# Normalised blocks at every second gate/up pair instead of at every pair, and two weight loads moved behind them

## The chip, the cores and the metric

One core of a Trainium2 chip runs the kernel. The metric is the device time of one execution in microseconds (us); of several executions the median is quoted.

In profile lines PE is TensorE and PEld its weight loads, DVE VectorE, ACT ScalarE, POOL GpSimd, and SPq the queue that issues DMA transfers. A line of a timeline gives start and length in us; a line of a group gives the busy time in us and, behind it, the mean ns of one instruction. `ps` is PSUM, to which TensorE writes its results, and `SB` is SBUF, the other memory of the core. Taking a result out of PSUM is called an evacuation.

## The reference, cut to what matters

A block of linear attention and a gated feed-forward block share one normalised input of 2048 tokens by 1024 features.

```python
xn = _layernorm(x)
pq, pk = phi(q), phi(k)                      # q, k, v = split(xn @ wqkv), 32 heads
kv, z = einsum(pk, v), einsum(pk)
num, den = pq @ kv, pq @ z + 1e-6
s = (num / den) @ wo
g = silu((silu(xn @ w_gate) * (xn @ w_up)) @ w_down)    # w_gate, w_up: 1024 x 3584
return x + s * g
```

The kernel divides not the product but phi(q) by its denominator, ahead of the product. This is "normalising PQ".

## The kernel before: the parts that matter here

The kernel lists its operations in program order; a scheduler written in the kernel then picks the order on each of five queues from modelled times and sets all semaphores. Its model lets a VectorE operation without an input in PSUM start only when GpSimd is free (`if o.port: when = max(when, free["pool"])`), but it adds no semaphore for that. After the q, k and v stage come 28 gate/up *pairs* (14 slices of the weights, each with two halves of the tokens; TensorE works 11.49 us on one), then the s stage and the d stage (down projection). Everything is multiplied by Strassen's scheme, so besides TensorE much adding and subtracting is to be done: VectorE and ScalarE take results out of PSUM, GpSimd combines the weights of coming slices.

PQ lies in eight blocks (token half `p`, a further half `j`, four of the eight head groups). One block is normalised so:

```python
def normalise(p, j, half):
    RBs = [tmp(F2), tmp(F2)]
    ...
    for hl in range(4):                 # reciprocals of the denominators, from DRAM
        ...  dma(...).pad = 3.0
    for g2 in range(2):
        RB = RBs[g2]
        for gl in range(2):             # four times: ScalarE scales, VectorE multiplies
            ...
            act([z_r] + [...], [RB], zr, zr, ACT.Identity, 512, "sb", scale=zc[:, g:g + 1])
            tt([sr, RB], [sr], src.bitcast(FP16), src, zr, ALU.mult, 512, True, NE[half])
    ...
    dma([SB.reg(o, 4 * KB)], [...], q_scr[p, half, j], ...)     # the block back to DRAM
```

The pairs, and what is listed with them:

```python
order = [(n, p) for n in range(12) for p in range(2)] + [(12, 0), (13, 0), (12, 1), (13, 1)]
norm = {N0 + q: [(q % 4 // 2, q % 2, q // 4)] for q in range(8)}        # N0 = 4
...
for z, (n, p) in enumerate(order):
    ...
    gu_pair(p, n, G[n], at)
    ...
    if z == N0 + 9:                     # down weights, into the room that PQ had
        wd_load("A10", 30.0)
        wd_load("A11", 30.0)
    if p == 0 and n < 12:               # once in two pairs: load and combine weights
        while wk[0] - 2 <= n + NA:
            next_load()                 # slice n + 2: DMA, then GpSimd
        G[n + 1].inner(IE, JG)          # GpSimd
    ...
    for a in norm.get(z, ()):
        normalise(*a)
```

So pair z is the first of the two that share a slice where z is even, and the second where z is odd, up to pair 23.

## Time and profile before

| | before |
|---|---|
| median of the runs beside the prediction | 744.12 us (740.38 to 744.96) |
| span of the profiled execution | 741.6 us |
| TensorE busy in the span | 706.9 us |

In the timeline of TensorE, kernel before (start, length), the figures in brackets are the idle time just before a stretch and what ended it.

```profile
257.26 1.91 PE L427 MATMUL ps<-SB 128*128 128x256 f16 x12 [1.78 <-ACT SB L477]
260.23 17.52 PE L427 MATMUL ps<-SB 128*128 128x512 f16 x112 [1.06 <-DVE ps L485]
279.18 11.32 PE L427 MATMUL ps<-SB 128*128 128x256 f16 x70 [1.43 <-DVE SB L485]
291.09 19.69 PE L427 MATMUL ps<-SB 128*128 128x256 f16 x128 [0.59 <-DVE SB L485]
...
333.35 148.76 PE L427 MATMUL ps<-SB 128*128 128x256 f16 x958 [1.29 <-ACT ps L477]
```

### The profile page before, as it was taken

To read this page: it belongs to the slowest core of one execution; us is meant where nothing else is said; L and a number is where in the kernel's file an instruction comes from. 1 tells how busy PE (TensorE), PEld (TensorE's weight loads), DVE (VectorE), ACT (ScalarE), POOL (GpSimd) and SP (SyncE) were. 2 spreads that over 40 slices of the span, in tenths; PEclk is the share of its full clock that TensorE was granted. 3 is DMA by queue.
4 is the path that set the end of the run, shared out by engine and by line. 5 is a ranking of instruction groups with operands and counts; after the bars stand their busy time and mean duration, and the time that the engine had idled before them with its cause. 6 is when DMAs were issued, how large, how long until landed. Compare 5 with 4: busy or idle time off the path is not lost.

```text
span 741.6 us, 11805 instructions
## 1 busy us (share of the span) xinstructions
PE 706.9 (95%) x4219; PEld 399.4 (54%) x4247; DVE 560.0 (76%) x1099; ACT 374.0 (50%) x729; POOL 286.2 (39%) x258
## 2 busy tenths in 40 slices
PE   8999999988899899999999999999999999999996
PEld 3444445544466555556666666666554456464642
DVE  6988776968977889888777777779878966556433
ACT  4777755976646576665455454454565112121211
POOL 2011000336558765983979767732840000000000
PEclk9999999999999999999999999999999999999999
DMA  9344245130233455358531334345699256573522
GB/s 302 99 81 102 44 113 170 59 114 4 78 102 97 135 178 190 121 159 287 174 100 46 112 93 121 94 130 163 213 278 282 87 171 186 168 206 95 184 72 71
DMA packets 142235, 101.58 MB, mean 137 GB/s; under 512 B 19040, under 2 KB 137056, under 8 KB 142176
## 3 DMA queue, kind: packets, MB, share of 16 engines
q1 hardware_dynamic: 142176, 100.82, 45.4%
q8 instruction: 33, 0.54, 0.3%
q14 instruction: 26, 0.21, 0.1%
HBM read 68.16 MB, written 29.49 MB: 132 GB/s over the span
## 4 chain that ended last, share of the span: by engine, by line
PE 73%; DVE 15%; DMA 6%; ACT 3%; issue 2%; SPq 0%; DVEq 0%; ACTq 0%
PE ps L427 73%; DVE SB L485 8%; ACT SB L477 3%; DMA SB<-h_scratch 2%; DMA SB<-SB 2%; DVE ps L485 2%; DVE SB L1041 1%; DVE SB L1048 1%; DMA SB<-in_A_x_dram 1%; DMA SB<-q_scratch 1%; DVE stats L1001 1%; ACT ps L477 1%; DVE stats L1002 1%; SPq L497 0%; DVE SB L1213 0%
## 5 line engine op out<-in xcount | busy, mean ns | idle before, releaser
L427 PE MATMUL ps<-SB 128*128 128x256 f16 (+4 forms) x4098 | 697.5, 331 | 24.8 <-ACT ps L477 7.0
L427 PEld LDWEIGHTS ps<-SB 128*128 128x128 f16 (+1 forms) x4126 | 393.7, 98 | 326.1 <-DVE ps L485 14.6
L485 POOL TENSOR_TENSOR SB<-SB 128x512 f16<-128x512 f16 (+5 forms) x224 | 272.2, 1250 | 200.8 <-PE ps L427 77.9
L477 ACT ACTIVATE SB<-ps 128x256 f32<-128x256 f32 (+5 forms) x443 | 233.8, 562 | 169.4 <-PE ps L427 154.6
L485 DVE TENSOR_TENSOR SB<-SB 128x512 f16<-128x512 f16 (+9 forms) x332 | 206.7, 658 | 58.6 <-ACT SB L477 18.6
L485 DVE TENSOR_TENSOR SB<-ps,SB 128x512 f16<-128x512 f32 (+2 forms) x318 | 182.0, 593 | 68.6 <-PE ps L427 53.0
L485 DVE TENSOR_TENSOR ps<-ps,SB 128x512 f32<-128x512 f32 (+1 forms) x250 | 128.2, 528 | 34.6 <-PE ps L427 28.1
L477 ACT ACTIVATE ps<-ps 128x512 f32<-128x512 f32 (+1 forms) x172 | 84.4, 491 | 104.8 <-PE ps L427 98.0
L477 ACT ACTIVATE SB<-SB 128x512 f16<-128x512 f32 (+1 forms) x68 | 42.2, 621 | 81.3 <-DVE SB L485 81.2
L1005 POOL TENSOR_TENSOR rstd<-veps,neg_half 128x1 f32<-128x1 f32 x16 | 11.4, 724 | 65.5 <-DVE veps L1004 64.3
L1041 DVE TENSOR_SCALAR SB<-SB 128x512 f16<-128x512 f16 x64 | 22.1, 353 | 9.3 <-ACT SB L477 9.3
L477 ACT ACTIVATE SB<-SB,zc 128x512 bf16<-128x512 bf16 x32 | 22.0, 717 | 4.5 <-DVE SB L485 3.7
L477 ACT ACTIVATE SB<-SB,nmr,rstd 128x1024 f16<-128x1024 bf16 x12 | 14.7, 1237 | 1.3 <-DVE nmr L1007 1.1
L1001 DVE BATCH_NORM_STATS2 stats<-SB 128x6 f32<-128x512 bf16 x16 | 11.0, 686 | 3.4 <-DMA SB<-in_A_x_dram 3.4
L1048 DVE SCALAR_TENSOR_TENSOR SB<-SB 128x512 bf16<-128x512 f32 x15 | 12.5, 843 | 0.0
L1002 DVE BATCH_NORM_STATS2 stats<-SB 128x6 f32<-128x512 bf16 x16 | 10.9, 681 | 0.0
L427 PE MATMUL ps<-SB,ident 128*128 128x512 f16 x17 | 5.7, 496 | 1.4 <-POOL ident L508 1.4
L1048 DVE SCALAR_TENSOR_TENSOR SB<-ps,SB 128x512 bf16<-128x512 f32 x9 | 6.1, 686 | 0.0
L456 PE MATMUL ps<-ident,SB 128*128 128x128 f16 x40 | 3.1, 220 | 2.3 <-DVE SB L1011 1.6
L456 PEld LDWEIGHTS ps<-ident,SB 128*128 128x128 f16 x40 | 2.4, 98 | 4.3 <-DVE SB L1011 2.8
L1298 DVE RECIPROCAL SB<-SB 128x64 f32<-128x64 f32 x8 | 4.4, 547 | 0.1
L427 PEld LDWEIGHTS ps<-SB,ident 128*128 128x128 f16 x17 | 1.9, 121 | 4.2 <-issue 2.2
(28 smaller groups left out, 23.5 us busy)
## 6 DMA issues: line engine op xcount, KB each, us to landing
h_scratch<-SB SPq DMA_DIRECT2D x112, 128.0 KB, 2.7
SB<-h_scratch SPq DMA_DIRECT2D x16, 896.0 KB, 6.2
SB<-in_B_w_gate_dram SPq DMA_DIRECT2D x14, 512.0 KB, 4.1
SB<-in_B_w_up_dram SPq DMA_DIRECT2D x14, 512.0 KB, 5.3
SB<-in_B_w_down_dram SPq DMA_DIRECT2D x4, 1792.0 KB, 9.0
SB<-in_A_wqkv_dram SPq DMA_DIRECT2D x12, 512.0 KB, 7.1
SB<-in_A_x_dram SPq DMA_DIRECT2D x16, 256.0 KB, 3.0
SB<-r_scratch SPq DMA_DIRECT2D x32, 128.0 KB, 2.8
```

Of the source, the lines that this page charges most:

```text
L427: last = h.matmul(o() if callable(o) else o, l() if callable(l) else l, r() if callable(r) else r, start=st, stop=sp, skip_group_check=True)
L456: last = h.transpose(o(), i(), ident[:, :])
L477: return op("act", reads, writes, lambda h: h.activation(ev(o), ev(i), func, **kw), n / 1200.0 + (0.055 if src == "ps" else 0.095) + (0.09 ...
L485: f = lambda h: h.tensor_tensor(ev(o), ev(a), ev(b), alu)
L1001: dve([xr] + ([named("ve", 0)] if q == 1 else []), [sA], lambda h: h.bn_stats(stats[:, j, 0, :], xa[:, 0:512]), 512)
L1002: dve([xr] + ([named("ve", 0)] if q == 1 else []), [sB], lambda h: h.bn_stats(stats[:, j, 1, :], xa[:, 512:1024]), 512)
L1005: pool([ver, nh_r], [rsr], lambda h: h.tensor_tensor(rstd[:, j, :], veps[:, j, :], neg_half[:, :], ALU.pow), 0.56)
L1041: dve([e], [e], lambda h: h.tensor_scalar(vap(e, FP16), vap(e, FP16), 1.0, EPS_PHI, ALU.min, ALU.add), 512, 3.84, urgent=PU).port = True
L1048: dve(reads + [e], [out_r], lambda h: h.scalar_tensor_tensor(out_ap, ev(src), 0.0, vap(e, FP16), ALU.max, ALU.add), 512, urgent=PU).port = ...
L1298: dve([ea], [ra], lambda h, q=q: h.reciprocal(vap(ra, F32)[:, q * 64:q * 64 + 64], vap(ea, F32)[:, q * 64:q * 64 + 64]), 400)
```

## The change

The intent is to thin out the extra work of VectorE and ScalarE: each block has two pairs to itself. The down weights, which take PQ's place, can then only be loaded later.

```diff
-    N0, NA, WA, QU, ZD = 4, 2, True, 20.0, 2
+    N0, NA, WA, QU, ZD, NS = 4, 2, True, 20.0, 2, 2
...
-        norm = {N0 + q: [(q % 4 // 2, q % 2, q // 4)] for q in range(8)}
+        norm = {N0 + NS * q: [(q % 4 // 2, q % 2, q // 4)] for q in range(8)}
...
-            if z == N0 + 9:
+            if z == N0 + NS * 7 + 2:
```

## The prediction

> **What bounds the kernel now.** I read the page first (who is busy), then the busy times by stretch, then TensorE's waits, and last the timelines of VectorE, GpSimd and the DMA queue side by side, because the question is what comes just before a TensorE gap. In the page, TensorE is the bound:
>
> ```profile
> PE 706.9 (95%) x4219; PEld 399.4 (54%) x4247; DVE 560.0 (76%) x1099; ACT 374.0 (50%) x729; POOL 286.2 (39%) x258
> ```
>
> The multiplications stay the same under the change, so all it can win is TensorE's idle time, 741.6 - 706.9 = 34.7 us in the whole span, and only the part that normalisation causes. The first line of the next block is the stretch that holds all eight normalised blocks (pairs 4 to 11, from the first reload of the reciprocals at 232 to the last stores at 336), the second the rest of the gate/up stage without them. The columns are busy time and count by engine:
>
> ```profile
> 232.00:338.00 106.00, 99.08 (x634) 60.94 (x633) 91.23 (x168) 68.85 (x134) 76.63 (x61) 1.00 0.49 155
> 338.00:440.00 102.00, 102.00 (x659) 64.27 (x657) 76.02 (x144) 49.96 (x107) 76.01 (x61) 1.00 0.45 141
> ```
>
> TensorE is full without the normalising and loses 6.92 us with it, at the same clock. The waits of TensorE in the first stretch add up to 2.0 + 1.8 + 1.8 + 1.3 = 6.9 us and all name VectorE or ScalarE; in the second there are none:
>
> ```profile
> PE ps L427 <- DVE SB L485: 2.0, 2, 1.4
> PE ps L427 <- DVE ps L485: 1.8, 3, 1.1
> PE ps L427 <- ACT SB L477: 1.8, 1, 1.8
> PE ps L427 <- ACT ps L477: 1.3, 1, 1.3
> ```
>
> A second measure that does not rely on modelled matmul ends is the issue of each gate weight, once for every two pairs, which waits for a buffer that TensorE gives back. Start, length, engine:
>
> ```profile
> 237.30 0.40 SPq L497 DMA_DIRECT2D SB<-in_B_w_gate_dram  x1
> 337.52 0.38 SPq L497 DMA_DIRECT2D SB<-in_B_w_gate_dram  x1
> 360.51 0.38 SPq L497 DMA_DIRECT2D SB<-in_B_w_gate_dram  x1
> 383.49 0.38 SPq L497 DMA_DIRECT2D SB<-in_B_w_gate_dram  x1
> ```
>
> Without normalising two pairs take 22.99 us (360.51 - 337.52; 22.98 for the next). From 237.30 to 337.52 there are four such periods in 100.22 us; 4 x 22.985 = 91.94. The loss is **8.28 us**, a little more than the visible idle time. That is what stands to be won.
>
> Why does normalising cost so much? Its 32 VectorE multiplications are one row of the list of groups in that stretch:
>
> ```profile
> L485 DVE TENSOR_TENSOR SB<-SB 128x512 f16<-128x512 bf16 x32 | 25.2, 822 | 0.0
> ```
>
> 822 ns is a mean of two very different cases. Single ones, in order of time (VectorE), and below them GpSimd's busy stretches:
>
> ```profile
> 239.50 0.75 DVE L485 TENSOR_TENSOR SB<-SB 128x512 f16<-128x512 bf16 x2
> 241.23 0.41 DVE L485 TENSOR_TENSOR SB<-SB 128x512 f16<-128x512 bf16 x1
> ...
> 252.47 3.25 DVE L485 TENSOR_TENSOR SB<-SB 128x512 f16<-128x512 bf16 x2
> 257.36 2.20 DVE L485 TENSOR_TENSOR SB<-SB 128x512 f16<-128x512 bf16 x2
> ```
>
> ```profile
> 227.77 10.40 POOL L485 TENSOR_TENSOR SB<-SB 128x1024 f16<-128x1024 bf16 x10
> 244.66 15.43 POOL L485 TENSOR_TENSOR SB<-SB 128x1024 f16<-128x1024 bf16 x11 [6.48 <-DMA SB<-in_B_w_up_dram]
> ```
>
> Block one (pair 4) falls at 239.5 to 242.3, where GpSimd is idle (238.17 to 244.66, waiting for the next up weights): 0.38 to 0.42 us each. Block two (pair 5) falls into GpSimd's 15.43 us stretch: 5.45 us for four. Over all eight blocks I count 16 multiplications in GpSimd's idle time, 6.24 us together (0.39 each), and 16 in its stretches, 18.96 us (1.19 each); the sum is the row's 25.2. Every one of the seven TensorE gaps (257.26, 260.23, 279.18, 291.09, 311.02, 311.95, 333.35) ends within about 5 us of a slow group (252.47, 257.36, 274.95, 286.95, 308.14, 328.19); no gap follows the fast groups of 239.5, 267.9, 292.6 to 295.3 and 335.3 before a slow one.
>
> **What the Trainium skill says.** "SBUF — State Buffer", section "Who interferes with whom": a VectorE instruction with two SBUF inputs contends with a GpSimd instruction that reads SBUF, and the one that issues second blocks fully until the first is through. The trace agrees: 0.39 us against 1.19 us for one form, split by whether GpSimd works. The same section has it that VectorE operations with at most one SBUF input do not contend, which fits the evacuations out of PSUM keeping their length with and without normalising (128x512 f32 to f16: 684 ns in the first stretch, 688 in the second). "VectorE: DVE Perf Modes", section "The perf-mode tier table", gives tensor_tensor on 16-bit SBUF operands the 2x mode and any PSUM operand 1x; 0.39 us here against 0.69 us for the PSUM form of the same size agrees in order. "Perfetto Trace Analysis", section "Per-instruction lifecycle", note on the GPSIMD instruction, warns that a GpSimd span is unreliable; I use only where its stretches begin and end, and the VectorE lengths confirm them.
>
> **The change part by part.** Nothing is added or removed: 8 blocks of 4 reciprocal reloads (128 KB each), 4 ScalarE scalings, 4 VectorE multiplications and one 512 KB store before and after; and two down loads of 1792 KB each.
>
> *Normalising at pairs 4, 6, ..., 18.* (a) Average load. A pair takes 11.49 us. Without a block VectorE does 8.5 us in it (17.02 in 360 to 383, halved) and ScalarE 5.7. A block adds 4 x 0.717 = 2.9 us on ScalarE and 1.6 to 6 us on VectorE. Before, eight pairs in a row carry one; VectorE was busy 91.23 of 106 us (86%) with the backlog handed from pair to pair. After, each loaded pair is followed by an empty one. (b) Position, which I hold to be the larger part. All even pairs are the first of their two, and GpSimd repeats its work once for every two. The instruction order of the changed kernel shows it: on the DMA queue each of the eight blocks has one and the same place, reloads, gate, two stores, up, one store, then the store of the normalised block, before GpSimd's combination of the just issued weights. This is the position of block one in the kernel before (reloads 231.96, gate 237.30, up 238.85, store 242.34). In the later stretch without normalising GpSimd ends a short group at 386.11 and starts the next weights at 390.69, with the gate issued at 383.49; the block should fall at about 385.7 to 388.8, idle but for perhaps the end of one 1.16 us operation. So the 32 multiplications should take 32 x 0.39 = 12.5 us instead of 25.2, and 8.5 + 1.6 = 10.1 of 11.49 us on VectorE, 5.7 + 2.9 = 8.6 on ScalarE in a loaded pair. That such a pair costs TensorE nothing is not only argued: from 232 to 247 the kernel before carries block one, and TensorE is busy 15.00 of 15.00 us. Gain on the path: the 8.28 us.
>
> *Down loads with pair twenty.* They must wait for the last normalised store, as the loaded bytes take its place. Before, one was issued between the gate and up weights and the other behind them (338.18 and 346.21), and the combination on GpSimd started only at 350.68, 13.2 us after the gate, against 7.2 normally; TensorE still had no gap. After, both lie three stores ahead of the gate of pair 24, about 10 us (418 to 429 in the old times). At the 279 to 288 GB/s moved by the DMA around 340, 3.67 MB take about 13 us, so the weights come some 3 us late: less than the 6 before, which cost nothing. They are first used in the s stage, well over 50 us later. Effect 0.
>
> *Later stages.* The s and d stages only start earlier. Their instruction order changes in a few places near the end; TensorE has 0.5 us of waits after 534 and cannot win there. I allow 0 to 1 us loss.
>
> Sum: -8.3 + 0 + 0.3 = -8 us; 744.1 - 8 = 736.
>
> **The rivals.** (1) The slow multiplications stay: what counts is that a block meets GpSimd's long work, and the scheduler's modelled times put it a few us off. For it: its margin is about 2 us. Against: block one and the repeated order. Then half of them or more are slow, gaps fall only through the lower average load, and I would see 740 to 742. (2) Average load alone is the cause and position is incidental: the gain would be about the same if an empty pair clears each backlog, but the multiplications would stay near 0.8 us. (3) The down loads back to back fill the queue, the stores of h behind them hold their buffers, and pairs 20 to 23 stall: 338.18 and later show one store waiting 3.33 us to be issued, yet no gap; 1 to 3 us lost, 737 to 739. (4) The gain is hidden again, as the s stage waits for transfers (3.9 and 4.6 us for q_scratch in the chain). Against: those loads are released by buffers that the same TensorE stream frees, so they move with it. If wrong, 739 to 744.
>
> **Range and chances.** The three times of before differ by 4.6 us, with the median near the top, so 736 has about 1.5 us of doubt from that alone; (1), (3) and (4) lengthen the upper side, nothing makes the gain much greater than the 8.3 us. I give 733 to 740.5. Faster by over 2% needs 729.2, a gain of 14.9 us, almost twice what this stage loses: 0.02. Slower by over 2% needs a new wait of 15 us: 0.01. Within 2%: 0.97.
>
> **What would show it.** Right: gate issues 23.0 us apart through pairs 4 to 19, no TensorE waits there, the 32 multiplications at 12 to 14 us in all, TensorE full from about 204 to 468, and later stages of the same length. Wrong: multiplications still near 800 ns (position failed); periods of over 23.5 us; a gap at pairs 20 to 23 beside the down loads; or a longer span from the last gate issue to the end.

## The result, and the profile after

The changed kernel took 734.01 us (731.7 to 736.4, 4 runs) against 743.46 us of the kernel before in the same rounds. The ratio is 0.9878, with a 95% interval of 0.9833 to 0.9924. A ratio here is the mean time of one kernel's runs over that of the other's of the same rounds, so not quite the ratio of the medians. Two more sets of runs gave 0.9904 and 0.9887; the mean of the three is 0.989, which is 8.2 us of 743.

Of the kernel after, in the order in which the prediction looked at the kernel before: the busy line of the page; the stretch from the first to the last block (busy time and count on TensorE, weight load, VectorE, ScalarE and GpSimd); the row of the 32 multiplications.

```profile
PE 705.0 (97%) x4247; PEld 400.0 (55%) x4247; DVE 546.9 (75%) x1099; ACT 372.3 (51%) x729; POOL 283.2 (39%) x258
```

```profile
228.00:404.00 176.00, 176.00 (x1137) 111.11 (x1136) 137.34 (x278) 105.86 (x215) 131.56 (x106) 1.00 0.45 142
```

```profile
L485 DVE TENSOR_TENSOR SB<-SB 128x512 f16<-128x512 bf16 x32 | 12.6, 415 | 0.0
```

TensorE is never idle while blocks are normalised, at the same granted clock of 1.00 as before, and the multiplications take half of what they took, with nothing changed in the instruction itself. One block on VectorE, and the stretches of GpSimd ahead of and behind it:

```profile
258.09 0.75 DVE L485 TENSOR_TENSOR SB<-SB 128x512 f16<-128x512 bf16 x2
259.82 0.42 DVE L485 TENSOR_TENSOR SB<-SB 128x512 f16<-128x512 bf16 x1
260.48 0.42 DVE L485 TENSOR_TENSOR SB<-SB 128x512 f16<-128x512 bf16 x1
```

```profile
239.94 17.56 POOL L485 TENSOR_TENSOR SB<-SB 128x1024 f16<-128x1024 bf16 x14 [6.17 <-DMA SB<-in_B_w_up_dram]
262.75 17.56 POOL L485 TENSOR_TENSOR SB<-SB 128x1024 f16<-128x1024 bf16 x14 [5.24 <-DMA SB<-in_B_w_up_dram]
```

GpSimd is idle from 257.50 (239.94 + 17.56) to 262.75, and the block lies from 258.09 to 260.90. The eight blocks follow each other at 22.98 to 22.99 us, and none of the 32 multiplications overlaps a GpSimd operation. Gate issues on the DMA queue:

```profile
232.91 0.40 SPq L497 DMA_DIRECT2D SB<-in_B_w_gate_dram  x1
255.89 0.40 SPq L497 DMA_DIRECT2D SB<-in_B_w_gate_dram  x1
...
439.76 0.38 SPq L497 DMA_DIRECT2D SB<-in_B_w_gate_dram  x1
```

Two pairs now take 22.98 us from the first block on. From 232.91 to the last gate issue it is 206.85 us; in the kernel before, the same distance (237.30 to 452.44) is 215.14 us. The difference is 8.29 us.

Read the spans with care. The profiled executions are 12.0 us apart (741.6 and 729.6), more than the change made. The table splits them at the first block's gate issue and at the last gate issue. The third column is another execution of the changed kernel.

| us | before | after | after, second set |
|---|---|---|---|
| start to the first block's gate issue | 237.30 | 232.91 | 237.32 |
| from there to the last gate issue | 215.14 | 206.85 | 206.85 |
| from there to the end | 289.1 | 289.8 | 291.2 |

The first row differs by 4.4 us between two executions of one kernel, before any instruction that was moved; the last by 1.4 us. A part of the 4.4 us goes with the clock: in 120 to 180 us it was 1.00 in the execution of the second column and 0.97 in the other two, by estimate 1.8 us (0.03 of 60 us). The rest is not explained. Only the middle row repeats to 0.01 us, and it holds the effect.

### The profile page after: what moved, and what is told of

It is laid out like the page before. It is cut to its first block, busy times and chain, and to the rows that moved or that the text cites.

```text
span 729.6 us, 11830 instructions
## 1 busy us (share of the span) xinstructions
PE 705.0 (97%) x4247; PEld 400.0 (55%) x4247; DVE 546.9 (75%) x1099; ACT 372.3 (51%) x729; POOL 283.2 (39%) x258
## 4 chain that ended last, share of the span: by engine, by line
PE 80%; DVE 8%; DMA 6%; ACT 3%; issue 1%; SPq 0%; DVEq 0%
PE ps L427 80%; DVE SB L485 4%; DMA SB<-h_scratch 3%; ACT SB L477 2%; DMA SB<-in_A_x_dram 1%; DMA SB<-q_scratch 1%; DVE SB L1041 1%; DVE ps L485 1%; DVE SB L1048 1%; DMA out_dram<-SB 1%; ACT ps L477 1%; SPq L497 0%; DMA SB<-SB 0%; DVE SB L1213 0%; DVE stats L1001 0%
## 5 line engine op out<-in xcount | busy, mean ns | idle before, releaser
L427 PE MATMUL ps<-SB 128*128 128x512 f16 (+4 forms) x4126 | 695.6, 330 | 15.6 <-ACT ps L477 4.7
L485 POOL TENSOR_TENSOR SB<-SB 128x512 f16<-128x512 f16 (+5 forms) x224 | 269.2, 1238 | 193.9 <-DMA SB<-in_B_w_up_dram 85.1
L485 DVE TENSOR_TENSOR SB<-SB 128x512 f16<-128x512 f16 (+9 forms) x332 | 193.1, 615 | 56.8 <-ACT SB L477 20.9
```

The lines of the kernel that those rows point to most:

```text
L427: last = h.matmul(o() if callable(o) else o, l() if callable(l) else l, r() if callable(r) else r, start=st, stop=sp, skip_group_check=True)
L485: f = lambda h: h.tensor_tensor(ev(o), ev(a), ev(b), alu)
```

## The experiments

Two theories stood against each other at the start. *Position*: a block costs TensorE time where its multiplications run beside GpSimd's work. *Load*: what counts is that a loaded pair is followed by an empty one. A third claim was that the down loads matter. Twelve runs were made, in three sets of four; the ratio is to the kernel before of the same set.

| run | what | median us | ratio (95% interval) | 32 multiplications, us |
|---|---|---|---|---|
| after_again | the changed kernel | 735.30 | 0.9904 (0.9879 to 0.993) | 12.7 |
| odd_pairs | blocks at pairs 5, 7, ..., 19 | 748.86 | 1.0084 (1.0059 to 1.0109) | 33.8 |
| two_per_even | two blocks at 4, 6, 8, 10 | 751.31 | 1.0118 (1.009 to 1.0147) | 24.5 |
| load_only | before, down loads at pair 20 | 743.85 | 1.0012 (0.9978 to 1.0045) | 24.8 |
| before_memset | before, GpSimd reads nothing | 725.69 | 0.9771 (0.9747 to 0.9794) | 12.2 |
| after_memset | after, GpSimd reads nothing | 724.77 | 0.9754 (0.973 to 0.9778) | 12.6 |
| six_on | blocks at pairs 6, 8, ..., 20 | 733.06 | 0.9877 (0.9851 to 0.9902) | 12.6 |
| load_late | after, down loads at pair 26 | 735.38 | 0.9901 (0.9875 to 0.9927) | 12.6 |
| odd_memset | odd_pairs, GpSimd reads nothing | 725.02 | 0.9763 (0.9736 to 0.9789) | 12.0 |
| two_memset | two_per_even, GpSimd reads nothing | 725.29 | 0.9769 (0.9746 to 0.9793) | 12.3 |
| xe2_pool | after, four more operations on GpSimd | 741.98 | 1.0 (0.9971 to 1.003) | 12.6 |
| after_third | the changed kernel | 734.11 | 0.9887 (0.9865 to 0.991) | 12.6 |

**The changed kernel as a control**, in two of the sets; no edit.

> Control, the changed kernel beside the variants. Every theory: ratio to the kernel before about 0.988 (some 734 against 743 us), no TensorE gap between the first and the last normalised block, the 32 multiplications 12.6 us together, gate issues 22.98 us apart.

> Control beside the three: ratio to the kernel before 0.986 to 0.993.

Both ratios came as expected.

**The same spread, at odd pairs** (edit to the changed kernel):

```diff
-    N0, NA, WA, QU, ZD, NS = 4, 2, True, 20.0, 2, 2
+    N0, NA, WA, QU, ZD, NS = 5, 2, True, 20.0, 2, 2
```

> Same spread over sixteen pairs, but each block at the second pair of its two (pairs 5, 7, ..., 19), down loads with pair 21. Position theory (a block must meet GpSimd's idle time): the multiplications fall into GpSimd's 17.56 us stretch, take 25 to 38 us together, TensorE gaps return, time 737 to 743. Load theory (an empty pair after each loaded one is enough): no gaps whatever the multiplications cost, time as the changed kernel, 733 to 735.

The spread is as wide as in the changed kernel, yet it was slower than the kernel before, and slower than even the position theory had it: 748.86 us. One block of it, on GpSimd, VectorE and TensorE in turn:

```profile
268.43 15.45 POOL L485 TENSOR_TENSOR SB<-SB 128x1024 f16<-128x1024 bf16 x11 [5.55 <-DMA SB<-in_B_w_up_dram]
```

```profile
276.52 2.98 DVE L485 TENSOR_TENSOR SB<-SB 128x512 f16<-128x512 bf16 x2
279.42 1.34 DVE L485 TENSOR_TENSOR SB<-ps,SB 128x256 f32<-128x256 f32 x3
```

```profile
280.89 23.43 PE L427 MATMUL ps<-SB 128*128 128x256 f16 x148 [1.36 <-ACT ps L477]
```

Two multiplications take 2.98 us instead of 0.75 inside GpSimd's stretch; the evacuations behind them on VectorE begin at 279.42. ScalarE's next two scalings waited 0.89 and 0.57 us for VectorE, so its evacuation too comes late (280.46), and TensorE, which by the profile waits for that one, stands for 1.36 us. The same gap follows every one of the eight blocks, 1.03 to 1.89 us. By the gate issues (236.45 to 434.98) eight periods take 198.53 us against 8 x 22.98 = 183.84: a loss of 14.7 us with 24 slow multiplications, where the kernel before loses 8.3 with 16. The load theory alone is refuted: an empty pair behind each loaded one saved nothing here.

**Two blocks at each of four even pairs** (edit to the changed kernel):

```diff
-        norm = {N0 + NS * q: [(q % 4 // 2, q % 2, q // 4)] for q in range(8)}
+        norm = {N0 + NS * q: [(r % 4 // 2, r % 2, r // 4) for r in (2 * q, 2 * q + 1)] for q in range(4)}
```

> Two blocks in each of pairs 4, 6, 8 and 10, none in the odd ones: the mean load of the kernel before with the position of the changed one. Position theory: the first block of a pair fast, the second running late into GpSimd's stretch, multiplications 14 to 20 us together, time 735 to 739. Load theory: two blocks on one pair are worse or no better than one on each, time 742 to 747.

Both expectations were missed: 751.31 us. The scheduler did not keep the second block in the pair; it let multiplications run on into GpSimd's stretch (three at 250.76 took 3.62 us, four at 272.15 took 4.71). Four periods, 235.49 to 346.71, took 111.22 us against 91.92, a loss of 19.3 us, though the multiplications together were no slower than in the kernel before. Their sum is thus no measure of the loss. The four periods, and below them the same four of two_memset (told of further down), with the length, then TensorE's busy time, and its granted clock third from the end:

```profile
235.49:346.71 111.22, 101.16 (x594) 59.53 (x593) 87.06 (x161) 64.53 (x128) 71.56 (x56) 0.92 0.45 144
```

```profile
227.86:320.51 92.65, 92.65 (x594) 57.09 (x593) 75.11 (x161) 64.38 (x128) 30.51 (x56) 1.00 0.55 172
```

For the same 594 matmuls TensorE was idle for 10.1 us (four gaps of 1.96 to 3.29) and busy for 8.5 us more, at a mean clock of 0.92: nearly half of the loss is TensorE at a lower clock, which was 0.64 to 0.71 in the 5 us from 255, 275, 305 and 340, around the ends of the four gaps. In odd_pairs, with gaps of at most 1.89 us, and in the kernel before the clock was 1.00 through the blocks. What lowers it is not shown.

**Only the down loads moved** (edit to the kernel before):

```diff
-            if z == N0 + 9:
+            if z == 20:
```

> The kernel before with only its two down loads moved to pair 20. Position and load theory: nothing, ratio to the kernel before 0.997 to 1.003 (743 us), gate issues as uneven as before between pairs 4 and 11. If the move of the loads gave a part of the gain: 735 to 741.

Nothing, as expected: 1.0012. The profile has the old gaps in the old places, for instance

```profile
257.24 1.91 PE L427 MATMUL ps<-SB 128*128 128x256 f16 x12 [1.14 <-ACT SB L477]
```

**The cause taken away.** In the kernel before and the changed one, and later in the two variants, every tensor_tensor of GpSimd was made a memset of the same output. Order, semaphores and all places stay; the result is wrong.

```diff
             if eng == "pool":
+                f = lambda h: h.memset(ev(o), 0.01)
                 return op("pool", reads, writes, f, n / 531.0 + 0.2)
```

> The kernel before, with every GpSimd tensor_tensor replaced by a memset of the same output (wrong result on purpose): same instruction order, semaphores and places of the blocks, but GpSimd reads nothing. Contention as cause: the 32 multiplications fall from 25.2 to about 12.5 us although one block still lies in every pair, the TensorE gaps between 232 and 337 go, and the time is within 1.5 us of the changed kernel with the same memsets. Load theory: VectorE's backlog comes from eight loaded pairs in a row, so gaps of some us stay and the time is at least 4 us above the changed kernel with memsets.

> The changed kernel with the same memsets (wrong result on purpose). Every theory: multiplications 12.5 us, no gaps in the gate/up stage, time as the changed kernel within 2 us (733 to 736).

> The odd-pair variant with every GpSimd tensor_tensor replaced by a memset (wrong result on purpose): blocks in the same places, GpSimd reads nothing. Contention as the cause of the loss of 1.0 to 1.9 us per block: all eight gaps go, multiplications about 12.5 us, time within 1.5 us of the changed kernel with memsets (some 725 us, ratio 0.974 to 0.978). If the second pair of two is bad for another reason, such as ScalarE or the stores: gaps of 1 us or more per block stay and the time is 4 us or more above.

> Two blocks in each of four even pairs, with memsets (wrong result on purpose). Its loss with contention was 19 us over four pairs, more than the slow multiplications alone would explain. If contention is all: gaps go, 725 us. If the load of one pair counts as well (ScalarE 5.7 + 2 x 2.9 = 11.5 us of 11.49, VectorE 8.5 + 3.2 = 11.7): 1 to 2 us per such pair stay, 729 to 733 us.

All four placements give the same time, 724.77 to 725.69 us, where with GpSimd's real work they lie 16 us apart. The expectation of after_memset was missed: it named the time of the changed kernel, 733 to 736 us. In the kernel before with memsets, eight loaded pairs stand in a row and no gap is left between 225 and 415 us (TensorE busy 190.00 of 190). Its multiplications, and GpSimd's new instructions in that stretch:

```profile
L485 DVE TENSOR_TENSOR SB<-SB 128x512 f16<-128x512 bf16 x32 | 12.2, 416 | 0.0
```

```profile
L487 POOL MEMSET SB<- 128x1024 f16 x32 | 29.7, 952 | 51.0 <-DMA SB<-in_B_w_up_dram 51.0
```

So eight blocks in four pairs, in eight pairs in a row or in every second of sixteen, even or odd, cost TensorE next to nothing as long as GpSimd does not hold VectorE up. Two blocks on one pair do leave a trace of load: four periods of two_memset (227.86 to 320.51) take 92.65 us, 0.7 more than 91.92. Of the 19.3 us above, 18.6 were thus lost only with GpSimd's real work.

A memset reads nothing, and it is also over two times as short (952 ns for 128x1024 against 2.13 us), so GpSimd was busy 62 us of 190 instead of 140. The times of these runs do not separate the two, but single instructions in the traces do. In the kernel before, each of the 16 slow multiplications began while a GpSimd operation was under way and ended 0.28 to 0.29 us after that operation; so did the 24 slow ones of odd_pairs and the 11 of two_per_even. In before_memset and two_memset nine multiplications began with 0.17 to 0.47 us of a memset still to run, and none took more than 0.42 us. One of each, kernel before and before_memset:

```profile
254.29 1.15 POOL L485 TENSOR_TENSOR SB<-SB 128x512 f16<-128x512 f16 x1
254.35 1.37 DVE L485 TENSOR_TENSOR SB<-SB 128x512 f16<-128x512 bf16 x1
```

```profile
271.25 0.53 POOL L487 MEMSET SB<- 128x512 f16 x1 [3.84 <-DVE SB L485]
271.44 0.42 DVE L485 TENSOR_TENSOR SB<-SB 128x512 f16<-128x512 bf16 x1
```

The first multiplication ends at 255.72, GpSimd's operation at 255.44; the second is through in 0.42 us beside a memset that lasts until 271.78. So in these traces a GpSimd operation that reads holds the multiplication up, and one that only writes does not. That GpSimd's results merely came too late is unlikely, since in the whole kernel before VectorE's additions and multiplications waited 0.6 us for GpSimd, and no TensorE wait of this stretch names it. Memsets also make the q stage faster: the gate issue at the first block comes at 225.25 to 227.86 in them, against 232.91 to 237.32 in the kernels before and after. That is why these kernels are 9 us below the changed one, and why they are to be compared with each other only.

**The spread one step later, and the down loads later still** (edits to the changed kernel):

```diff
-    N0, NA, WA, QU, ZD, NS = 4, 2, True, 20.0, 2, 2
+    N0, NA, WA, QU, ZD, NS = 6, 2, True, 20.0, 2, 2
```

> Blocks at pairs 6, 8, ..., 20, down loads with pair 22: again the first pair of each two, one step later. Position theory and load theory: as the changed kernel, 733 to 735, multiplications 12.6 us. Only if it were the particular pairs or the time left for the down loads that counted would it differ.

```diff
-            if z == N0 + NS * 7 + 2:
+            if z == 26:
```

> The changed kernel with the down loads issued with pair 26, next to the first loads of the s stage. If the place of the down loads is of no account: 733 to 736. If they need the distance they have: DMA waits in the s stage, 737 to 742.

Both took as long as the changed kernel. It is not pair 4 that is good but the even place, and the down loads have room to spare: issued from 478.6 us on, within the s stage, they still caused no wait that the profile shows.

**A use of the finding elsewhere.** Just ahead of the first pair, two VectorE operations take 3.26 us beside GpSimd's work (195.27 us in the profile after) and TensorE then stands for 2.03 us. I meant to give that group to GpSimd (edit to the changed kernel):

```diff
-    XE0 = XE1 = XE2 = XE3 = "dve"
+    XE0 = XE1 = XE3 = "dve"; XE2 = "pool"
```

> The changed kernel with the four combinations of inputs that end just ahead of the first gate/up pair given to GpSimd instead of VectorE, where two of them took 3.26 us beside a GpSimd operation and a TensorE gap of 2.03 us follows. Contention theory: the gap shrinks or goes, up to 2 us won, 732 to 735. If GpSimd's own queue delays its next work as much, nothing or a loss: 735 to 739.

The edit moved another group, and the expectation shares the mistake. VectorE's form 128x512 f16 from f16 falls from 72 operations to 68, and GpSimd's rises from 56 to 60. The two slow ones have a bf16 output and are, by the kernel's code, additions of phi; their form stays at 72 on VectorE, and here such a pair took 2.66 us (197.90 below). So this run does not test what it was meant to test.

It lost the whole gain, 741.98 us, worse than the loss I had named. The blocks stayed fast; the loss lies before them: the gate issue at the first block comes at 242.89 us. In the q stage, on VectorE and TensorE:

```profile
193.79 4.19 DVE L1041 TENSOR_SCALAR SB<-SB 128x512 f16<-128x512 f16 x2
197.90 2.66 DVE L485 TENSOR_TENSOR SB<-SB 128x512 bf16<-128x512 f16 x2
```

```profile
201.22 13.23 PE L427 MATMUL ps<-SB 128*128 128x512 f16 x74 [5.11 <-DVE SB L485]
```

GpSimd's first stretch grew from 17.18 to 20.53 us, and its next one (193.59 to 199.95) now met other VectorE work. Tensor_scalar instructions, with one input in SBUF and 0.28 us each when free (187.49 us in the same profile), took 4.19 us for two, and TensorE stood for 5.11 us, after 4.71 us at 181.12. Its granted clock was 0.94 in 180 to 240 us, against 1.00 in the profile after, so a part of the loss is slower work. That the moved operations shifted GpSimd into this is argued from one trace. No version with a right result beat the changed kernel clearly; six_on is equal to it within the intervals.

## Why the prediction was right

- *Time.* 736 was predicted, 734.01 us measured, inside 733 to 740.5. The gain is 1.2%, within the 2% to which the prediction gave 0.97. Most of the 2 us may lie in the base: the first three runs of before had a median of 744.12, eleven in each later set 742.3 to 743.0.
- *The size of the loss to be won.* 8.28 us by the gate periods; 8.29 us by the trace, 8.2 us by the mean ratio. TensorE was to be full from about 204 to 468 us, and was.
- *Position over load.* The multiplications were to fall to 12.5 us and fell to 12.6, all in GpSimd's idle time. That position was the cause, and not the thinner load, had been argued from the pattern of one kernel; the odd pairs, with the same spread and 14.7 us lost, and the memset runs, with four placements and one time, show it. One slow group in the pattern (282.77, 1.47 us) had no gap behind it, which the prediction passes over. The prediction gave load a part as well. That part is too small to be seen in the changed kernel: with memsets the dense kernel was 0.9 us above the spread one, and their periods were equal. So the change as it was meant, to thin out the load, would not have helped at odd pairs. That the first block's pair (4) was an even one was luck as far as that intent goes, though not for the prediction, which named the place.
- *Down loads.* Effect 0 was right. The weights of pair 24 were to be some 3 us late; GpSimd began on them at 424.47, 7.7 us after their gate issue, against 6.9 to 7.3 in the periods around it, so at most 0.8 us late. The term was over-estimated: the down loads were issued 10.8 us ahead of that gate, and the slowest one of the execution landed 11.9 us after its issue.
- *Rivals.* (1) Slow multiplications did not happen here, but the odd pairs show what they cost. (2) Load alone is refuted. (3) Nothing stalled at pairs 20 to 23. (4) The gain was not hidden later: from the last gate issue to the end it took 289.1 us before, 289.8 after, and 289.1 to 292.1 over all fourteen profiled executions.

## What to carry to other kernels

Before thinning out work on a busy engine, split the lengths of one and the same instruction by what the other engines do at that time: two clear groups (0.39 and 1.19 us here) point to a contention, and then *where* the work lies can decide, as it did here, and not how densely. Spreading by an even step beside a periodic neighbour fixes the phase for good or ill: the same spread gained 8 us at even pairs and lost 6 at odd ones. After an edit, count the operations of each form on each engine: that shows whether the edit moved what it was to move. Compare profiled executions stage by stage from a common event, since their spans differed by 12 us where the change made 8.

## What the Trainium skill lacked or had wrong

- "SBUF — State Buffer", "Who interferes with whom": its rule held (two SBUF inputs on VectorE against a reading GpSimd instruction). It puts it as a question of who issues first; what it lacks is that against a GpSimd queue that runs without pause it was nearly always VectorE that lost: of the 17 multiplications that overlapped a GpSimd operation in the kernel before, 16 had begun behind it. Those 16 took 1.19 us instead of 0.39, while GpSimd's own operations were in the mean at most 39 ns longer than in the changed kernel (128x1024: 2133 and 2125 ns; 128x256: 705 and 670, and 712 and 673). Right behind a slow multiplication GpSimd lost more: 1.34 us at 257.94, where the same form took 1.15 us at 254.29.
- The same section: that ScalarE never waits for anyone agrees with the runs (the scalings took 717 ns before, 711 ns after). That a GpSimd instruction which only writes does not hold up VectorE's two-input form agrees with the memset runs: nine multiplications that began with at least 0.17 us of a memset to run took 0.42 us at most.
- "Perfetto Trace Analysis", "Optimizing Scalar/DVE Operations", warns that moving work between GpSimd and VectorE might not help. Here it could well be stronger: four operations moved cost 8 us (742.0 against 734.1).
- No page that bears on this says by how much the profiled spans of one program can differ before the first changed instruction: 4.4 us between two executions of the changed kernel.
